# Attention's exponentials transposed by VectorE and a round trip through DRAM instead of by TensorE, for units 20 to 31

## The chip, the cores and the metric

The kernel runs on one core of one Trainium2 chip. The metric is the device time of one execution in microseconds, lower is better. Engines are named as in the profile: PE is TensorE's matrix multiply, PEld its weight load, DVE is VectorE, ACT is ScalarE, POOL is GpSimd, SP is SyncE, which issues all transfers of the kernel before.

## The reference

Three layers follow each other; all is float32 at the boundary. The change is in the first.

```python
# attention: q, k, v are (8 batches, 8 heads, 576 tokens, 64)
k_p = k.reshape(B, H, 72, 8, D).mean(axis=3)
v_p = v.reshape(B, H, 72, 8, D).mean(axis=3)
scores = scale * np.matmul(q, k_p.transpose(0, 1, 3, 2))
scores = scores - np.max(scores, axis=-1, keepdims=True)
attn = np.exp(scores)
attn = attn / (np.sum(attn, axis=-1, keepdims=True) + 1e-09)
attn_out = np.matmul(attn, v_p)
# first feed-forward layer: x is (4608 tokens, 512)
h = x @ w_in                                    # 512 -> 2048
g = np.where(h > 0.0, h, np.exp(np.minimum(h, 0.0)) - 1.0)
x1 = g @ w_out                                  # 2048 -> 512
# second layer: 512 -> 1024 -> 512, a softmax gate and a layer norm between
```

## The kernel before

**Attention** works in 32 units, one for each batch and pair of heads. Unit `i` is batch `i // 4`, pair `i % 4`; the two heads of a pair lie on 128 partitions. A unit from 4 on goes through these helpers. `att_setup` (L176) pools keys and values: DVE reduces (`att_kr`, `att_vr`, the latter into tile `vr`), ACT scales (`att_kc`, `att_vc`). `att_scores` (L183) multiplies five tiles of 128 queries, which start at the tokens in `QT` (0, 128, 256, 384 and 448, so that the last two overlap), by the pooled keys: ten PE instructions, into two PSUM banks. `att_max` (L206) takes the row maximum on DVE and subtracts it into the tile `es`, 128 queries by 10 groups (tile and head) by 72 keys. `att_exp` (L215) is one ACT instruction on 720 columns. `att_soft` (L229) sums and inverts on DVE and multiplies on POOL (L241). `att_T` (L243) transposes with PE against the identity: `att_T(i, 0)` four transposes of the first head (L251), `att_T(i, 1)` four of the second and the two of the last tile (L256); ACT copies the results from PSUM into `a`, 72 keys by 2 heads by 576 tokens (L252, L258). `att_V` (L262) multiplies by the pooled values (L277), in two pieces since a batch of 576 tokens crosses a block of 512, and `att_x` (L280) copies to `xr` and stores in DRAM (`x0d`).

**Order of the work.** The first feed-forward layer sets the pace. Its tokens are in nine blocks of 512. The first three are done straight, in slots `(j, f)` (functions `m_h1` to `m_o1`), each slot with a piece of `w_out` that ACT rounds (`woh`) and POOL subtracts (`wol`, L560). The other six blocks are done in three pairs with seven products instead of eight (`h_step`, L842; `mul_o`, L902): first the products with `w_in` (PE L818), then those with `w_out` (PE L908), their operands `op` prepared by ACT (L898) and DVE (L899), and the weights read by SP into a ring of 14 buffers (`wr`, L810). Between these pieces `att_half` (L369) issues attention by quarters of a unit: quarter 0 is scores, maximum and exponentials of unit `i`; quarter 1 its sums and product, and the second half of the transposes of unit `i - 1`; quarter 2 the product with the values of unit `i - 1` and the setup of unit `i + 1`; quarter 3 the first half of the transposes of unit `i`. Units 20 and 21 fall at the end of the third straight block and the start of the first pair, 22 to 27 into the first pair, 28 to 31 into the second. In all this stretch the program's scheduler may move instructions on each engine; every engine then runs its own list strictly in that order. The start (four units, first conversions of weights) and the second layer are ordered by hand.

Tiles come from pools: a tag has `bufs` buffers, and a tile that takes a buffer waits until all users of the tile before it there are done. `es` has 3 buffers, `a` 2, `vr` 2.

Of the kernel before, what the change touches and what calls it, by code (L numbers as in the profile page):

```python
# [8 lines left out]
F32 = mybir.dt.float32  # L9
# [11 lines left out]
def kernel(  # L21
# [41 lines left out]
    w3d = dr.tile([P, 7, NF // 2, 2, 256], F32, name="w3d")  # L63
    w2d = dr.tile([P, 7, 4, 512], F32, name="w2d")
    o2d = dr.tile([P, 2, 2, 4, 512], F32, name="o2d")
    zd = [dr.tile([4, P, 256], F32, name=f"zd{i}") for i in range(4)]
    ident = cst.tile([P, P], F32, name="ident")
    make_identity(nc, ident)
# [18 lines left out]

    GROUPED = (1, 2)
    NTREE = 3

    xh, xl = {}, {}
    gate = {}
# [71 lines left out]

    def att_vr(i):
        v_t = st["kq", units[i][1]][2] if i < NP else st["ld", i][1]
        vr = st["vr", i] = pa.tile([SK, P], F32, name=f"vr{i}", tag="vr")
        if i < NTREE:
            pool_tree(vr, v_t)
        else:  # L170
            nc.vector.tensor_reduce(vr, v_t, axis=AX, op=ALU.add)
# [8 lines left out]
    def bc(x, m):  # L180
        return x.rearrange("p (a o) -> p a o", o=1).to_broadcast([P, m, SK])

    def att_scores(i, banks):  # L183

        kp, vt = st["kp", units[i][0], units[i][1]]
        q_t = st.pop(("q", i))
        st["sv", i] = []
        for t0, t1 in ((0, 2), (2, 4)) if i < NP else ((0, 3), (3, 5)):
            s = next(banks)
            ts = QT[t0:t1]  # L190
            for t, o in enumerate(ts):
                nc.tensor.matmul(  # L192
                    s[:, t * 2 * SK:(t + 1) * 2 * SK], q_t[:, o:o + P], kp, start=True, stop=True
                )
            m = 2 * len(ts)
            st["sv", i].append((2 * t0, m, s[:, 0:m * SK].rearrange("p (a k) -> p a k", k=SK)))
            yield
        st["a", i] = (pa.tile([P, NG, SK], F32, name=f"es{i}", tag="es", bufs=3), vt)

    def grouped(i):  # L200
        return i in GROUPED
# [4 lines left out]
    def att_max(i):  # L206
        es, vt = st["a", i]
        mx = st["mx", i] = small(f"mx{i}")
        for g0, m, sv in st["sv", i]:
            mxs = mx[:, g0:g0 + m]  # L210
            nc.vector.tensor_reduce(mxs, sv, axis=AX, op=ALU.max, negate=grouped(i))
            if not grouped(i):
                nc.vector.tensor_tensor(es[:, g0:g0 + m, :], sv, bc(mxs, m), op=ALU.subtract)

    def att_exp(i):  # L215
# [27 lines left out]
    def att_T(i, h):  # L243

        es, vt = st["a", i]
        if h == 0:
            st["aT", i] = pa.tile([SK, 2, S], F32, name=f"a{i}", tag="a")
        a = st["aT", i]
        pt = ps.tile([P, 512], F32, name=f"pt{i}_{h}", tag="C")
        for t in range(4):  # L250
            nc.tensor.transpose(pt[0:SK, t * P:(t + 1) * P], es[:, 2 * t + h, :], ident)  # L251
        nc.scalar.copy(a[:, h, 0:4 * P], pt[0:SK, :])  # L252
        if h == 1 and i >= NP:
            pr = ps.tile([P, 512], F32, name=f"pr{i}", tag="C")
            for g in range(2):
                nc.tensor.transpose(pr[0:SK, g * P:(g + 1) * P], es[:, 8 + g, :], ident)  # L256
            lo = 5 * P - S
            nc.scalar.copy(  # L258
                a[:, :, 4 * P:S], pr[0:SK, 0:2 * P].rearrange("s (g t) -> s g t", g=2)[:, :, lo:P]
            )  # L260

    def att_V(i, banks):  # L262


        b, p = units[i]
        es, vt = st.pop(("a", i))
        a = st.pop(("aT", i))
        j = b * S // 512
        n = 512 * (j + 1) - b * S
        st["pv", i] = []  # L270
        for o, w, blk, at in ((0, n, j, b * S - 512 * j), (n, S - n, j + 1, 0)):
            if i < NP and o:
                continue
            pv = next(banks)
            for h in range(2):
                d = slice(64 * h, 64 * h + 64)
                nc.tensor.matmul(pv[d, 0:w], vt[:, d], a[:, h, o:o + w], start=True, stop=True)  # L277
            st["pv", i].append((pv[:, 0:w], blk, slice(at, at + w)))

    def att_x(i):  # L280
# [31 lines left out]
    def rest(part):  # L312

        kz = st["kz"]
        if part == 0:
            s = ps.tile([P, 512], F32, name="rs", tag="C")
            for p in range(NP):
# [1 line left out]
                    s[RW * (p % 2):RW * (p % 2) + RW, (p // 2) * 2 * SK:(p // 2 + 1) * 2 * SK],  # L319
                    kz[:, p, qr], kz[:, p, 0:2 * SK], start=True, stop=True,  # L320
                )
            es = st["rest"] = pa.tile([P, NG, SK], F32, name="esr", tag="es", bufs=3)[:, 0:NP]
            mx = small("mxr")[:, 0:NP]
            sv = s[:, 0:NP * SK].rearrange("p (a k) -> p a k", k=SK)
            nc.vector.tensor_reduce(mx, sv, axis=AX, op=ALU.max)
# [43 lines left out]
    def att_half(n):  # L369

        while nload[0] < min(NU, n // 4 + 3):
            att_load(nload[0])
            nload[0] += 1
        i, r = divmod(n, 4)
        before = NP <= i - 1
        if r == 0:
            if i < NU:
                for _ in att_scores(i, single()):
                    pass
                att_max(i)  # L380
                att_exp(i)
        elif r == 1:
            if i < NU:
                att_soft(i)
            if before:
                att_T(i - 1, 1)
        elif r == 2:
            if before:
                att_V(i - 1, single())
                att_x(i - 1)  # L390
            if i + 1 < NU:
                att_setup(i + 1)
        elif r == 3:
            if i < NU:
                att_T(i, 0)


# [1268 lines left out]
```

## Time and profile before

| | us |
|---|---|
| median of three runs (lowest, highest) | 1268.59 (1268.41, 1273.28) |
| profiled execution, own time | 1271.26 |
| its span in the trace | 1269.7 |
| PE busy | 1241.9 (98%) |
| PEld busy | 994.5 (78%) |
| DVE busy | 988.7 (78%) |
| ACT busy | 825.9 (65%) |
| POOL busy | 176.3 (14%) |

The span is the time from the first to the last instruction of the program on the slowest core; the execution's own time holds 1.6 us more that lies around it. Times inside the trace count from the start of the span. A matrix product's row shows how long one instruction took from start to end; they overlap in the pipeline, so the pace is read from the distance of starts. Between the third straight block and the last unit's product with the values lie 366 to 700 us.

### The profile page before, as it was taken

The numbers are of one execution on the slowest core, as the hardware profiler recorded it, in microseconds if no ns is written. First come the engines' busy times: TensorE is split into PE (matmuls) and PEld (weight loads), VectorE is DVE, ScalarE is ACT, GpSimd is POOL, SyncE is SP. The second block draws the span as 40 slices with busy tenths as digits, with TensorE's granted clock in tenths as the row PEclk, the third lists the DMA queues.
The fourth block names the chain that finished last, engine by engine and source line by source line (L and its number), as shares of the span: only waits on it lengthen the run. The fifth ranks groups of instructions, "written<-read, shape, count | busy, mean of one in ns | idle before, by whom it ended". The sixth has DMA issues, their size and how long they took to land.

```text
span 1269.7 us, 17261 instructions
## 1 busy us (share of the span) xinstructions
PE 1241.9 (98%) x5768; PEld 994.5 (78%) x5768; DVE 988.7 (78%) x1484; ACT 825.9 (65%) x1405; POOL 176.3 (14%) x148
## 2 busy tenths in 40 slices
PE   8999999999999999999999999999799999999998
PEld 6777877777777878788888777888688888888887
DVE  7898688978877799776795767986778787877763
ACT  7887566666656784557764477754667676767664
POOL 4564222333310001100000000000000000000000
PEclk8999999999999999999999999999899999999999
DMA  9976366665758877796666888878364444545451
GB/s 305 311 213 200 126 216 223 211 223 166 239 192 276 260 214 241 216 310 191 210 210 208 273 264 258 284 261 288 124 185 158 138 155 147 176 140 158 125 157 42
DMA packets 177065, 263.30 MB, mean 207 GB/s; under 512 B 16465, under 2 KB 96849, under 8 KB 175953
## 3 DMA queue, kind: packets, MB, share of 16 engines
q1 hardware_dynamic: 176976, 262.21, 65.0%
q8 instruction: 46, 0.75, 0.2%
q14 instruction: 43, 0.34, 0.1%
HBM read 182.46 MB, written 79.69 MB: 206 GB/s over the span
## 4 chain that ended last, share of the span: by engine, by line
PE 81%; DVE 8%; DMA 6%; ACT 3%; issue 1%; POOL 0%; SPq 0%; DVEq 0%; ACTq 0%; POOLq 0%
PE po L1138 15%; PE hA L818 13%; PE oA L908 12%; PE o L694 8%; PE h L639 8%; PE zX L1007 7%; PE zZ L1007 4%; PE at L192 3%; PE oB L908 3%; PE at L277 2%; PE hB L818 2%; PE pt L251 2%; PE zY L1007 2%; DMA w2d<-cv 1%; DMA x1r<-x1d 1%
## 5 line engine op out<-in xcount | busy, mean ns | idle before, releaser
L1138 PE MATMUL po<-w,dhl 128*128 128x512 f32 x864 | 204.5, 393 | 0.0
L908 PE MATMUL oA<-op,wr 128*128 128x512 f32 x864 | 202.4, 392 | 0.0
L908 PEld LDWEIGHTS oA<-op,wr 128*128 128x128 f32 x864 | 160.8, 188 | 38.1 <-issue 2.9
L1138 PEld LDWEIGHTS po<-w,dhl 128*128 128x128 f32 x864 | 162.7, 189 | 35.4
L898 ACT CAST op<-g 128x1024 fp32r<-128x1024 f32 x84 | 87.9, 1050 | 70.4 <-PE oA L908 32.2
L899 DVE TENSOR_TENSOR op<-g,op 128x1024 fp32r<-128x1024 f32 x84 | 102.8, 1231 | 33.8 <-ACT op L898 33.4
L818 PE MATMUL hA<-sS,wr 128*128 128x512 f32 x432 | 108.8, 394 | 1.8 <-ACT sp L830 1.8
L1007 PE MATMUL zX<-w,xh 128*128 128x512 f32 x288 | 100.9, 392 | 1.4 <-ACT sn L1017 1.4
L1086 POOL TENSOR_TENSOR sc<-sc,mhalf 128x1 f32<-128x1 f32 x36 | 19.3, 549 | 579.1 <-DVE sc L1085 344.1
L560 POOL TENSOR_TENSOR wol<-wo,woh 128x512 fp32r<-128x512 f32 x48 | 74.0, 1542 | 174.6 <-ACT woh L559 167.7
L818 PEld LDWEIGHTS hA<-sS,wr 128*128 128x128 f32 x432 | 79.9, 188 | 21.4 <-ACT sp L830 3.2
L241 POOL TENSOR_TENSOR es<-es,sm 128x720 f32<-128x720 f32 x28 | 48.2, 1722 | 304.9 <-DVE sm L239 137.1
L639 PE MATMUL h<-xh,wh 128*128 128x512 f32 x192 | 79.5, 414 | 2.4 <-DVE e L656 2.4
L838 DVE SCALAR_TENSOR_TENSOR g<-ep,g 128x512 f32<-128x512 f32 x72 | 50.9, 713 | 34.5 <-ACT ep L837 34.3
L694 PE MATMUL o<-gh,woh 128*128 128x512 f32 x192 | 77.6, 404 | 0.0
L639 PE MATMUL h<-xh,wl 128*128 128x512 f32 x192 | 76.2, 397 | 0.0
L639 PE MATMUL h<-xl,wh 128*128 128x512 f32 x192 | 76.2, 397 | 0.0
L694 PE MATMUL o<-gh,wol 128*128 128x512 f32 x192 | 75.0, 391 | 0.0
L1119 DVE TENSOR_TENSOR dhl<-dT,dhl 128x1024 fp32r<-128x1024 f32 x32 | 39.2, 1225 | 41.2 <-ACT dhl L1115 41.2
L1007 PEld LDWEIGHTS zX<-w,xh 128*128 128x128 f32 x288 | 54.0, 188 | 14.6 <-ACT sn L1017 2.1
L836 ACT ACTIVATE ep<-g 128x512 f32<-128x512 f32 x72 | 44.8, 628 | 25.6 <-DVE g L870 13.3
L892 DVE TENSOR_TENSOR g<-g,g 128x1024 f32<-128x1024 f32 x48 | 61.3, 1290 | 0.1
(354 smaller groups left out, 2736.8 us busy)
## 6 DMA issues: line engine op xcount, KB each, us to landing
wr<-w1d SPq DMA_DIRECT2D x168, 256.0 KB, 3.8
wr<-w3d SPq DMA_DIRECT2D x168, 256.0 KB, 2.9
raw<-in_w SPq DMA_DIRECT2D x48, 512.0 KB, 5.7
dT<-zd SPq DMA_DIRECT2D x128, 128.0 KB, 3.1
v<-in_v SPq DMA_DIRECT2D x32, 288.0 KB
x1r<-x1d SPq DMA_DIRECT2D x9, 1024.0 KB, 5.4
out<-ot SPq DMA_DIRECT2D x36, 256.0 KB, 2.0
w1d<-ci SPq DMA_DIRECT2D x16, 512.0 KB, 2.9
```

Of the source, the lines that this page charges most:

```text
L241: eng.tensor_tensor(es, es, bc(sm, n), op=ALU.mult)
L560: nc.gpsimd.tensor_tensor(ol, t[:, f % 4, :], oh.bitcast(F32), op=ALU.subtract)
L639: nc.tensor.matmul(h[:, 0:n], a[g][:, kk, fo:fo + P], x[j][:, kk, 0:n], start=(kk == 0 and m == 0), stop=(kk == KDM - 1 and m == 2), skip_ ...
L694: nc.tensor.matmul(acc, a[:, dm * P:(dm + 1) * P], x[:, 0:n], start=(f == 0 and m == 0), stop=(f == NF - 1 and m == 2))
L818: nc.tensor.matmul(bank, w[:, a, kk], x[:, b, kk], start=(start and m == 0), stop=(stop and m == 5), skip_group_check=True,)
L838: gate["dve"] = nc.vector.scalar_tensor_tensor(d, e, 1.0, h, op0=ALU.subtract, op1=ALU.max).ins
L892: nc.vector.tensor_tensor(d, x, y, op=op)
L898: gate["act"] = nc.scalar.copy(o[:, 0], src).ins
L899: gate["dve"] = nc.vector.tensor_tensor(o[:, 1], src, o[:, 0].bitcast(F32), op=ALU.subtract).ins
L908: nc.tensor.matmul(banks[d], ws[i][:, a, d * P:(d + 1) * P], o[:, b, i], start=(start and t == 0 and i == 0 and m == 0), stop=(stop and t ...
L1007: nc.tensor.matmul(bank, x[:, o:o + P], w[:, y + k, :], start=(start and m == 0), stop=(stop and m == 5), skip_group_check=True,)
L1138: nc.tensor.matmul(po, a[:, c], b[c // 4][:, c % 4, :], start=(m == 0), stop=(m == 3 * NC2 - 1))
```

## The change

For units from `BLOCKT = 20` on the transposes leave PE. `att_T` isn't called. The exponentials are laid out in `es` with the head outermost, padded from 720 to 736 columns (23 blocks of 32; POOL sets the last 16 to zero). A new `att_D` lets DVE transpose each block of 32 by 32 in place and has POOL issue four transfers, one for each 32 partitions, that store the blocks to one of four DRAM tiles `ed`, 736 rows of 128 queries, in runs of 32 numbers (128 bytes, 736 of them in each transfer). A new `att_A` has POOL issue one transfer back, 720 rows of 512 bytes, into `a` as 72 keys by 10 groups by 128 queries. `a` grows from 576 to 640 columns a head, the ACT copies go, and the query tiles are chosen so that no tile crosses the border of a block (`qtiles`). `vr` goes from two buffers to one, for all units.

```diff
+    ed = [dr.tile([736, P], F32, name=f"ed{i}") for i in range(4)]
...
+    BLOCKT = 20
...
-        vr = st["vr", i] = pa.tile([SK, P], F32, name=f"vr{i}", tag="vr")
+        vr = st["vr", i] = pa.tile([SK, P], F32, name=f"vr{i}", tag="vr", bufs=1)
...
+    def border(i):
+        o = units[i][0] * S
+        return 512 * (o // 512 + 1) - o
+
+    def qtiles(i):
+        if i < BLOCKT:
+            return QT
+        m = -(-border(i) // P)
+        return [P * t if t < m else S - P * (5 - t) for t in range(5)]
...
-            ts = QT[t0:t1]
+            ts = qtiles(i)[t0:t1]
...
-        st["a", i] = (pa.tile([P, NG, SK], F32, name=f"es{i}", tag="es", bufs=3), vt)
+        e = st["ef", i] = pa.tile([P, 736], F32, name=f"es{i}", tag="es", bufs=3)
+        st["a", i] = (e[:, 0:NG * SK].rearrange("p (g k) -> p g k", k=SK), vt)
...
-            if not grouped(i):
+            if i >= BLOCKT:
+                t = slice(g0 // 2, (g0 + m) // 2)
+                nc.vector.tensor_tensor(
+                    es.rearrange("p (h t) k -> p t h k", h=2)[:, t], sv.rearrange("p (t h) k -> p t h k", h=2),
+                    mxs.rearrange("p (t h o) -> p t h o", h=2, o=1).to_broadcast([P, m // 2, 2, SK]), op=ALU.subtract,
+                )
+            elif not grouped(i):
...
-            st["aT", i] = pa.tile([SK, 2, S], F32, name=f"a{i}", tag="a")
+            st["aT", i] = pa.tile([SK, 2, 5 * P], F32, name=f"a{i}", tag="a")
...
+    def att_D(i):
+
+        e = st.pop(("ef", i))
+        nc.vector.transpose(e, e)
+        for b in range(4):
+            nc.gpsimd.dma_start(
+                out=ed[i % 4][:, 32 * b:32 * b + 32].rearrange("(c f) j -> f c j", f=32),
+                in_=e[32 * b:32 * b + 32].rearrange("f (c j) -> f c j", j=32),
+            )
+
+    def att_A(i):
+        a = st["aT", i] = pa.tile([SK, 2, 5 * P], F32, name=f"a{i}", tag="a")
+        nc.gpsimd.dma_start(
+            out=a.rearrange("k h (t q) -> k (h t) q", q=P), in_=ed[i % 4][0:NG * SK].rearrange("(g k) q -> k g q", k=SK)
+        )
...
-                nc.tensor.matmul(pv[d, 0:w], vt[:, d], a[:, h, o:o + w], start=True, stop=True)
+                c = o + (64 if o and i >= BLOCKT else 0)
+                nc.tensor.matmul(pv[d, 0:w], vt[:, d], a[:, h, c:c + w], start=True, stop=True)
...
         if r == 0:
+            if i - 1 >= BLOCKT:
+                att_A(i - 1)
             if i < NU:
                 for _ in att_scores(i, single()):
                     pass
+                if i >= BLOCKT:
+                    nc.gpsimd.memset(st["ef", i][:, NG * SK:], 0.0)
...
-            if before:
+            if before and i - 1 < BLOCKT:
                 att_T(i - 1, 1)
         elif r == 2:
+            if BLOCKT <= i < NU:
+                att_D(i)
...
-            if i < NU:
+            if i < BLOCKT:
                 att_T(i, 0)
```

How the built programs stand on three engines shows what waits behind what. Line numbers are each program's own: in the changed one the scores are L204, the product with the values L313, the product on POOL L260, the transpose L284, the stores L286, the load L293.

**POOL, units 22 to 26, before** (`es_4273` is unit 23):

```order
L241 TENSOR_TENSOR es_4057<-es_4057,sm_4105 128x720
L241 TENSOR_TENSOR es_4273<-es_4273,sm_4315 128x720
L241 TENSOR_TENSOR es_4483<-es_4483,sm_4526 128x720
L241 TENSOR_TENSOR es_4697<-es_4697,sm_4767 128x720
L241 TENSOR_TENSOR es_4904<-es_4904,sm_4949 128x720
```

and in the changed program, units 23 to 26 (`es_4260` is unit 23, `es_4666` unit 25, `es_4864` unit 26; `ed_79` holds unit 25):

```order
L260 TENSOR_TENSOR es_4260<-es_4260,sm_4303 128x720
L286 DMA ed_81<-es_4260 32x23x32 x4
L293 DMA a_4452<-ed_81 72x10x128
L419 MEMSET es_4461 128x16
L260 TENSOR_TENSOR es_4461<-es_4461,sm_4505 128x720
L286 DMA ed_78<-es_4461 32x23x32 x4
L293 DMA a_4657<-ed_78 72x10x128
L419 MEMSET es_4666 128x16
L260 TENSOR_TENSOR es_4666<-es_4666,sm_4737 128x720
L286 DMA ed_79<-es_4666 32x23x32 x4
L260 TENSOR_TENSOR es_4864<-es_4864,sm_4910 128x720
L293 DMA a_4855<-ed_79 72x10x128
```

Each load stands behind its unit's four stores, whose landing it waits for, and ahead of the next unit's product; only for unit 25 does the product of unit 26 stand between its stores and its load.

**DVE, unit 23, before:**

```order
L236 TENSOR_REDUCE sm_4315<-es_4273 128x10
L838 SCALAR_TENSOR_TENSOR g_3777<-ep,g_3777 128x512
L238 TENSOR_SCALAR sm_4315<-sm_4315 128x10
L156 TENSOR_REDUCE kr_4996<-k_4684 128x72
L239 RECIPROCAL sm_4315<-sm_4315 128x10
L870 TENSOR_TENSOR g_3776<-hA,sp 128x512
L859 TENSOR_TENSOR g_3772<-hB,sp 128x512
```

and in the changed program:

```order
L255 TENSOR_REDUCE sm_4303<-es_4260 128x10
L880 SCALAR_TENSOR_TENSOR g_3787<-ep,g_3787 128x512
L257 TENSOR_SCALAR sm_4303<-sm_4303 128x10
L912 TENSOR_TENSOR g_3786<-hA,sp 128x512
L258 RECIPROCAL sm_4303<-sm_4303 128x10
L901 TENSOR_TENSOR g_3782<-hB,sp 128x512
L284 STREAM_TRANSPOSE es_4260<-es_4260 128x736
```

The transpose stands one instruction behind the inversion that POOL's product waits for, and itself waits for that product; the feed-forward layer's own work is queued behind it.

**PE, unit 25, before** (`a_4859` is unit 25's transposed tile, `es_4697` its exponentials):

```order
L192 MATMUL at<-kpbd_87,q_4472 128x144 x5
L908 MATMUL oB<-op,wr 128x512 x24
L251 MATMUL pt_1_4954<-ident,es_4697 72x128 x4
L256 MATMUL pr_4960<-ident,es_4697 72x128 x2
L908 MATMUL oB<-op,wr 128x512 x12
L277 MATMUL at<-a_4859,vt_4590 64x128 x2
L277 MATMUL at<-a_4859,vt_4590 64x448 x2
```

and in the changed program, where `a_4855` is what unit 25's load brings:

```order
L204 MATMUL at<-kpbd_91,q_4448 128x144 x5
L950 MATMUL oB<-op,wr 128x512 x36
L950 MATMUL oA<-op,wr 128x512 x18
L313 MATMUL at<-a_4855,vt_4564 64x128 x2
L313 MATMUL at<-a_4855,vt_4564 64x448 x2
```

The transposes are gone; the product with the values stands 18 matrix products later than before behind the scores of the next unit. For the other units of the first pair it keeps its place.

## Rows read from the trace of the kernel before

**Rows 1.** Stretches: us, then each engine's busy us, granted clock, DMA share, GB/s.

```profile
462.00:542.00 80.00, 80.00 (x393) 63.27 (x392) 70.29 (x85) 45.50 (x75) 8.94 (x4) 1.00 0.73 228
...
366.00:700.00 334.00, 332.07 (x1588) 264.73 (x1586) 257.65 (x331) 212.41 (x362) 19.47 (x11) 1.00 0.75 235
```

**Rows 2.** Waits of PE from 366 to 705: total us, times, longest.

```profile
PE hB L818 <- DVE sP L735: 0.6, 1, 0.6
```

**Rows 3.** PE in order of time: start us, us, instruction.

```profile
405.20 1.52 PE L818 MATMUL hB<-sP,wr 128*128 128x512 f32 x6
406.57 0.60 PE L251 MATMUL pt<-ident,es 128*72 128x128 f32 x4
...
407.14 1.64 PE L818 MATMUL hA<-sA,wr 128*128 128x512 f32 x6
408.61 1.53 PE L818 MATMUL hA<-sV,wr 128*128 128x512 f32 x6
...
416.81 0.60 PE L251 MATMUL pt<-ident,es 128*72 128x128 f32 x4
417.17 1.62 PE L818 MATMUL hB<-sP,wr 128*128 128x512 f32 x6
418.62 1.52 PE L818 MATMUL hA<-sA,wr 128*128 128x512 f32 x6
```

**Rows 4.** POOL in order of time, the products of units 23, 25 and 26.

```profile
430.24 1.40 POOL L241 TENSOR_TENSOR es<-es,sm 128x720 f32<-128x720 f32 x1 [20.43 <-DVE sm L239]
...
476.67 2.16 POOL L241 TENSOR_TENSOR es<-es,sm 128x720 f32<-128x720 f32 x1 [24.47 <-DVE sm L239]
490.82 2.16 POOL L241 TENSOR_TENSOR es<-es,sm 128x720 f32<-128x720 f32 x1 [11.98 <-ACT a L258]
```

**Rows 5.** PE in order of time, the products with the values of units 23 and 25.

```profile
451.71 1.19 PE L277 MATMUL at<-a,vt 72*64 72x192 f32 x8
...
492.32 1.19 PE L277 MATMUL at<-a,vt 72*64 72x128 f32 x8
```

**Rows 6.** DVE's block transposes in the second layer: duration ns min/median/max.

```profile
L1095 DVE STREAM_TRANSPOSE hb<-e x16: 1234/1236/1236, 916.6 to 1226.8; 128x1024 f32<-128x1024 f32 x16
```

**Rows 7.** SP's issue of a weight transfer of 128 rows: ns min/median/max.

```profile
L810 SPq DMA_DIRECT2D wr<-w1d x168: 319/320/1019, 369.2 to 789.0; - x168
```

**Rows 8.** Transfers by way of DRAM in the second layer: KB each, us to landing.

```profile
dT<-zd SPq DMA_DIRECT2D x128, 128.0 KB, 3.1
```

**Rows 9.** POOL's product of attention: ns min/median/max.

```profile
L241 POOL TENSOR_TENSOR es<-es,sm x28: 1392/1401/2892, 63.1 to 657.1; 128x720 f32<-128x720 f32 x28
```

**Rows 10.** DMA queue from 402 to 442: packets, MB, share of 16 engines.

```profile
q1 hardware_dynamic: 5303, 10.07, 82.8%
```

**Rows 11.** The same from 1000 to 1200.

```profile
q1 hardware_dynamic: 27550, 31.40, 50.6%
```

**Rows 12.** The start, DVE in order of time.

```profile
25.58 1.20 DVE L171 TENSOR_REDUCE vr<-v 72x128 f32<-72x1024 f32 x1
26.82 1.53 DVE L434 TENSOR_SCALAR wo<-wo 128x1024 uint32<-128x1024 uint32 x1
```

**Rows 13.** The start, ACT in order of time.

```profile
26.68 0.30 ACT L174 ACTIVATE kz<-vr 72x128 f32<-72x128 f32 x1
```

**Rows 14.** The start, PE in order of time.

```profile
39.67 0.50 PE L639 MATMUL h<-xh,wh 128*128 128x512 f32 x1 [2.37 <-DVE e L656]
```

**Rows 15.** The first pair's start, DVE in order of time.

```profile
375.99 0.22 DVE L239 RECIPROCAL sm<-sm 128x10 f32<-128x10 f32 x1
376.86 1.97 DVE L757 TENSOR_TENSOR sw<-sP,su 128x1024 f32<-128x1024 f32 x1 [0.65 <-DMA x1d<-x1s]
```

**Rows 16.** POOL behind unit 20's product, at 334 to 341.

```profile
334.06 1.46 POOL L241 TENSOR_TENSOR es<-es,sm 128x720 f32<-128x720 f32 x1 [1.35 <-DVE sm L239]
339.06 1.29 POOL L560 TENSOR_TENSOR wol<-wo,woh 128x512 fp32r<-128x512 f32 x1 [3.54 <-ACT woh L559]
```

**Rows 17.** PE where that piece of `wol` is first used.

```profile
346.34 0.39 PE L694 MATMUL o<-gh,wol 128*128 128x512 f32 x1
```

More of the change, by code (lines that the diff above doesn't have):

```diff
@@ L321, in rest @@
                 )
-            es = st["rest"] = pa.tile([P, NG, SK], F32, name="esr", tag="es", bufs=3)[:, 0:NP]
+            es = st["rest"] = pa.tile([P, 736], F32, name="esr", tag="es", bufs=3)[:, 0:NP * SK].rearrange("p (g k) -> p g k", k=SK)
             mx = small("mxr")[:, 0:NP]
```

## The prediction

> **What bounds the kernel now.** I read the stretches first: from 366 to 700 us, where the changed units lie, PE is busy 332.07 of 334 us [rows 1], so a PE instruction taken away there is time taken away, as long as PE doesn't wait for something new. Then the waits: what other engines cost PE there is small, 0.6 us at the first pair's start the only one that lasts beyond the transposes [rows 2]. DVE has room over the stretch as a whole (257.65 of 334 us) but little in the middle: 70.29 of 80 us from 462 to 542 [rows 1]. POOL is nearly idle, 19.47 us of 334.
>
> **What goes.** I read PE in order of time to see what transposes take from it, since their own durations overlap. Six matrix products take 1.37 us (405.20 to 406.57). Behind the six transposes at 406.57 the next six begin at 407.14, 0.57 later, and need 1.47 instead of 1.37, so these transposes cost 0.67. The four at 416.81 cost 0.36 (to 417.17) and again 0.08 in the products behind them, so 0.44 [rows 3]. A unit's ten cost 1.11 us. Twelve units lose them; unit 20's lie where PE is about to wait for DVE anyway, and I count eleven: **-12.2 us**.
>
> The Trainium skill (TensorE: Matmul & The Clock Gate, Part 4: PE-mode transpose) gives about 275 ns for one transpose inside a kernel. As an estimate, ten at that price would be 2.75 us a unit and eleven units 30 us. The rows agree with 275 ns only as one instruction's time from start to end and show 111 ns as what PE loses, so the trace decides.
>
> ACT's three copies a unit go as well. Nothing waits for ACT in the rows that bound the stretch, so I count nothing. The padding on POOL (16 columns) and the other order of the subtraction (the same columns on DVE) I count at nothing too; the cover is POOL's idle time and DVE's room, and if it is gone they cost what the rival on DVE says.
>
> **What is added: a chain that must end before PE reaches the product with the values.** POOL's product starts at 430.24 for unit 23 and PE's product with the values at 451.71, 21.5 us later [rows 4, 5]. Without the 1.1 us of transposes between them 20.4 are left. The new chain:
>
> - POOL's product, 1.40 us [rows 9].
> - DVE's transpose. The second layer's takes 1.236 us for 1024 columns [rows 6], so 736 columns take 0.89; with half a microsecond behind DVE's own work, 1.4.
> - Four issues on POOL of 736 descriptors each. No row shows POOL issuing a transfer. Below: SP's issue of 128 rows, 0.32 us [rows 7]. Above: POOL goes through 720 columns in 1.40 us [rows 9], 1.95 ns a step; were each of a descriptor's four words such a step, 736 would take 5.7, with SP's 0.32 on top 6.1 us. I take one step a descriptor, 1.44 + 0.32 = **1.75 us**, since the row on POOL itself is the nearest. Four take 7.0.
> - The stores' landing, as for the second layer's round trip, 3.1 us [rows 8]; the load's issue, 1.75; its landing, 3.1.
>
> Sum 1.4 + 1.4 + 7.0 + 3.1 + 1.75 + 3.1 = 17.75 us. It fits into 20.4 with 2.7 to spare. Unit 25 is the exception. Its load stands behind unit 26's product on POOL, which starts at 490.82 and takes 2.16 [rows 4]; with 1.75 and 3.1 the data land at 497.8. PE's product with the values stood at 492.32 [rows 5], 18 products at 0.228 us later in the new order, so 496.4, and 0.7 earlier for the transposes that no longer stand between it and unit 26's scores: 495.7. PE waits **+2.1 us** there. Behind POOL's issues nothing urgent is queued in the first pair: zeros for a later unit, then the next product 20 us on. In the second pair the distances are longer. At unit 20 it is the pieces of `wol` that are queued: POOL's product starts at 334.06, so with 1.4 for it and 1.4 for DVE the issues run from 336.9 to 343.9; the piece that began at 339.06 and took 1.29 ends at 345.2, and PE uses it at 346.34 [rows 16, 17]. That just holds.
>
> **DVE waits with the transpose.** It stands one instruction behind the inversion, so DVE idles for most of POOL's product, and everything behind it on DVE is late by up to 1.4 + 0.9. At the first pair's start it costs: the inversion of unit 21 ends at 376.21, POOL's product and the transpose then hold DVE until about 378.6, where before `sw` started at 376.86 and took 1.97 beside POOL's product [rows 15]. Alone it takes about 1.2, so it ends at 379.8 instead of 378.83, and less the 0.44 us by which the scores are earlier, PE's existing wait for what comes after it [rows 2] grows by 0.5 to 1: **+0.8 us**. Elsewhere DVE's work is prepared ahead of PE and I count nothing; the price without that is below.
>
> **One buffer for `vr`.** At the hand-ordered start the fourth unit's reduction on DVE (25.58) must now wait for ACT's scaling of the third, which ends at 26.98 [rows 12, 13], 1.4 us. DVE's conversions are queued behind it, and PE waits 2.37 us for their end until 39.67 [rows 14]. Between 0 and 1.4; since the conversion at 26.82 took 1.53 us beside POOL's work and may then be alone, I take **+1.0**.
>
> **The transfers** add 377 KB of stores in 2944 pieces and 369 KB of loads in 720 a unit. From 402 to 442 the queue moved 10.07 MB in 5303 packets with 82.8% of 640 engine-us, 52.6 ns a KB; from 1000 to 1200 a packet of 1.14 KB took 58.8 ns [rows 10, 11]. By bytes a unit adds 39 engine-us, 2.5 us of all sixteen; with each piece as dear as those packets, 13.5. Packet time goes with size in these two rows (99.9 ns for 1.9 KB), so I take 4 us, a share of 20% where 17% is free in the worst 40 us and more elsewhere. The ring of 14 weight buffers covers that; the price without it is below.
>
> **Sum:** -12.2 + 2.1 + 0.8 + 1.0 = **-8.3 us**. The profiled execution took 1271.3 us, its span 1269.7 and 1.6 around it, so 1263.0 by it. It stands 2.7 above the median of the runs, 1268.6, to which the forecast is made: **1260.3 us**.
>
> **The rivals.**
>
> *POOL's issues take longer, and PE waits at the product with the values.* This one ends slower. It decides from 2.2 us an issue, where the 2.7 us to spare are used up by five issues; every further microsecond makes a unit 5 us late, and as a wait gives the next unit its time back, about half is paid, 15 us over six units. At 2.8 the gain is gone. From 3.2 on it is slower by over 0.5%, and near 3 the issues, 5 x 3 with a landing and a product, also fill the 20 us from unit to unit. At 4 us POOL needs 24.5 a unit where 19.2 pass, 5.3 too much for six units: about +30, **1290 us**; at 6.1 us over 1340. For it: 736 descriptors are many, and no row bounds them well. Against: POOL does nothing else.
> The Trainium skill (DMA: Bandwidth & Descriptors, Anatomy of one DMA) calls descriptor generation a small, variable part of a fixed cost of about 2.0 us of a transfer from GpSimd; by that, issues would be well below 2 us and this rival would not occur. No run here shows it yet.
>
> *DVE becomes the bound from 462 to 542 us.* It has 9.7 us free there [rows 1]; four units add 0.89 each and a wait for POOL's product of up to the 2.16 it takes there [rows 4], 12.2 in all. About 2.5 us don't fit, and PE loses them, with as much again where a late operand holds ACT: **1265 us**, no change that can be told. For it: DVE's share. Against: PE waited for DVE only once there.
>
> *The small pieces fill the transfer engines, and weights come late.* At 8 us a unit, two units add 16 us to 40 us with 6.9 free; over six units some 15 us of PE's waits would be left after the ring has given what it has: **1275 us**. From about 5 us a unit on it decides.
> The Trainium skill (DMA: Bandwidth & Descriptors, Specifications) asks for 512 bytes at least, below which a transfer reads, modifies and writes; by that the pieces of 128 bytes would be dearer than their bytes. In the trace no store is so small, so it doesn't speak either way.
>
> **How the numbers follow.** Forecast 0.46; DVE bound 0.18; transfers 0.10; POOL's issues 0.26, half of it above 1290. The low end, 1253, is all twelve units' 13.3 us and up to 2 us of late work on ACT that goes, with none of the small losses. The high end, 1290, takes in the DVE and transfer cases and POOL's up to 4 us an issue; about 0.13 lies above and 0.04 below. Cases of both signs hold chances; the forecast's own range is 1255 to 1262. A measurement of this kernel can tell about 0.5%, 6.3 us, from no change. Faster by more than that: the forecast and a little of the rivals' better ends, 0.47. Within it: DVE's case, the milder transfer case and issues between 2.4 and 3.2 us, 0.27. Slower: 0.26.
>
> **What would show it.** Right: no L251 and L256 rows in the changed lines for units 20 on, PE's busy time down by some 12 us in the stretch, POOL's issues near 1.75 us, the product with the values without a wait except at unit 25, DVE idle 1 to 2 us ahead of each transpose. Wrong: PE waiting for the loads of `a` at L313 again and again (POOL's issues or slow landings), weights waiting on `wr` (transfers), or `op` late (DVE). The start is right if PE's first wait for `e` ends about 1 us later than 39.67.

## Result: 1.2% slower, and the profile after

The changed kernel takes 1285.05 us (median of four runs, 1281.62 to 1287.14) against 1268.61 of the kernel before beside it. The ratio is 1.0118, 95% interval 1.0086 to 1.0150: slower by 15 us, where 8 us less were forecast.

| | before, us | after, us |
|---|---|---|
| profiled execution, own time | 1271.26 | 1284.97 |
| its span | 1269.7 | 1283.0 |
| PE busy | 1241.9 | 1236.3 |
| DVE busy | 988.7 | 995.4 |
| ACT busy | 825.9 | 813.1 |
| POOL busy | 176.3 | 222.3 |

PE has less to do and the span is longer, so PE waits. The stretches, which answer to [rows 1] (columns as there: PE, PEld, DVE, ACT and POOL busy, granted clock, DMA share, GB/s):

```profile
462.00:542.00 80.00, 73.96 (x337) 57.29 (x336) 62.54 (x81) 38.61 (x60) 20.31 (x24) 0.96 0.87 253
366.00:700.00 334.00, 314.63 (x1413) 247.72 (x1413) 255.94 (x337) 194.05 (x318) 62.58 (x75) 0.98 0.84 253
```

PE idles 19.4 us of 334 where it idled 1.9. DVE is *less* busy from 462 to 542 than before (62.54 against 70.29), so DVE's capacity is not the bound. The DMA share rose from 0.75 to 0.84. PE's waits from 402 to 572, where before there were none at all (what was waited for, us in total, times, longest):

```profile
PE at L313 <- DMA a<-ed: 5.9, 3, 3.5
PE oA L950 <- ACT sp L872: 5.3, 1, 5.3
PE hA L860 <- ACT sp L872: 1.8, 2, 1.4
```

Setting equal PE products of the two traces side by side shows where the time goes: after is 1.8 us late at 331 us, 3.4 at 373, back to 1.5 at 441 (the transposes that are gone), 7.2 at 505, 14.1 at 543, 16.2 at 587, and 12.9 to 13.0 from 804 to the end. (Each is one start in after less the same product's in before.) So the first pair's second half loses it in two steps.

**First step, unit 25**, POOL and then PE in order of time, which answer to [rows 4, 5]:

```profile
480.42 2.18 POOL L260 TENSOR_TENSOR es<-es,sm 128x720 f32<-128x720 f32 x1 [13.03 <-ACT xr L327]
483.89 2.92 POOL L286 DMA_DIRECT2D ed<-es  x4 [1.28 <-DVE es L284]
493.28 2.18 POOL L260 TENSOR_TENSOR es<-es,sm 128x720 f32<-128x720 f32 x1 [6.47 <-DVE sm L258]
495.42 0.92 POOL L293 DMA_DIRECT2D a<-ed  x1
```

```profile
493.52 4.24 PE L950 MATMUL oA<-op,wr 128*128 128x512 f32 x18
501.27 2.19 PE L313 MATMUL at<-a,vt 72*64 72x128 f32 x8 [3.51 <-DMA a<-ed]
503.39 6.24 PE L950 MATMUL oA<-op,wr 128*128 128x512 f32 x18
```

The load stands behind unit 26's product, as the prediction had it, and PE waits 3.51 us. Then the same 18 products that took 4.24 us take 6.24, and the eight with the values 2.19 instead of 1.19 [rows 5]. The stretches around them show why (clock is the third column from the end):

```profile
496.00:499.00 3.00, 1.76 (x8) 1.13 (x6) 3.00 (x4) 0.00 (x0) 2.60 (x5) 1.00 0.69 182
501.30:503.50 2.20, 2.20 (x9) 0.80 (x9) 2.20 (x3) 0.27 (x1) 0.00 (x0) 0.50 0.47 110
503.50:506.00 2.50, 2.50 (x6) 2.04 (x7) 1.55 (x2) 0.74 (x2) 1.01 (x2) 0.50 0.33 102
```

After PE stood still the granted clock is 0.50, the lower level (1.2 of 2.4 GHz): the wait of 3.5 us costs 3.0 us more. The wait below does it again (granted clock 0.54 from 548 to 552): 90 products take 22.85 us behind it, where at the pace of the run's other products (36 in 8.48) they take 21.2.

**Second step, 534 to 547**, DVE, ACT and PE in order of time:

```profile
540.00 0.75 DVE L158 TENSOR_REDUCE kr<-k 128x72 f32<-128x576 f32 x1 [5.63 <-DMA k<-in_k]
540.66 0.21 DVE L258 RECIPROCAL sm<-sm 128x10 f32<-128x10 f32 x1
...
543.23 0.95 DVE L284 STREAM_TRANSPOSE es<-es 128x736 f32<-128x736 f32 x1 [1.28 <-POOL es L260]
544.10 1.18 DVE L934 TENSOR_TENSOR g<-g,g 128x1024 f32<-128x1024 f32 x1
```

```profile
545.37 1.04 ACT L940 CAST op<-g 128x1024 fp32r<-128x1024 f32 x1 [8.05 <-DVE g L934]
...
546.48 0.59 ACT L872 COPY sp<-oA 128x512 f32<-128x512 f32 x1
```

```profile
547.12 22.85 PE L950 MATMUL oA<-op,wr 128*128 128x512 f32 x90 [5.33 <-ACT sp L872]
```

DVE waits for keys (unit 31's, by the order of its list; PE needs them only after 650 us). SP issued that load at 530.30, so it took 9.7 us until DVE could start:

```profile
530.30 0.38 SPq L123 DMA_DIRECT2D k<-in_k  x1
```

Before, the loads of keys from 402 to 572 us landed in 3.4 to 4.0 us (min/median/max):

```profile
DMA to landing us min/median/max: 3.4/3.8/4.0
```

While the late load was under way the transfer engines were full, at a DMA share of 1.03 (columns as in the stretches above):

```profile
530.00:540.00 10.00, 9.04 (x44) 6.74 (x42) 4.33 (x9) 2.74 (x5) 0.00 (x0) 1.00 1.03 235
```

Behind this wait, on DVE, stand unit 28's inversion, the transpose with its wait for POOL's product, then the feed-forward layer's sums; ACT waits for those, and the copy that frees PE's bank is queued on ACT.

**The landing**, stores and loads of the whole execution (issue ns min/median/max; us to landing min/median/max), which answer to [rows 8]:

```profile
L286 POOL DMA_DIRECT2D ed<-es x48: 727/728/924, 338.6 to 679.3; - x48
...
DMA to landing us min/median/max: 2.8/4.3/7.1
```

```profile
L293 POOL DMA_DIRECT2D a<-ed x12: 883/893/917, 350.8 to 685.4; - x12
...
DMA to landing us min/median/max: 5.7/7.4/10.3
```

**The load on the transfer engines**, POOL's queue from 402 to 700 us, ten units (packets, MB, share of 16 engines), which answers to [rows 10]:

```profile
q0 software_dynamic: 3360, 7.47, 12.2%
```

### The profile page after: what moved, and what is told of

Read it like the earlier page. It is cut to its first block, busy times and chain, and to the rows that moved or that the text cites. A ratio compares the mean times of both kernels' runs of the same rounds, so it can differ in the third digit from the quotient of the medians.

```text
span 1283.0 us, 17134 instructions
## 1 busy us (share of the span) xinstructions
PE 1236.3 (96%) x5648; PEld 986.4 (77%) x5648; DVE 995.4 (78%) x1496; ACT 813.1 (63%) x1369; POOL 222.3 (17%) x220
## 4 chain that ended last, share of the span: by engine, by line
PE 69%; DVE 11%; DMA 10%; ACT 5%; issue 2%; POOL 1%; SPq 1%; ACTq 0%; DVEq 0%; POOLq 0%
PE po L1180 15%; PE oA L950 11%; PE hA L860 9%; PE zX L1049 7%; PE o L736 7%; PE h L681 6%; PE zZ L1049 4%; DMA raw<-in_w 3%; PE at L204 2%; PE zY L1049 2%; PE oB L950 2%; PE hB L860 2%; DMA x0d<-xr 2%; PE at L313 1%; DMA a<-ed 1%
## 5 line engine op out<-in xcount | busy, mean ns | idle before, releaser
L950 PE MATMUL oA<-op,wr 128*128 128x512 f32 x864 | 205.4, 397 | 6.5 <-ACT sp L872 5.3
L950 PEld LDWEIGHTS oA<-op,wr 128*128 128x128 f32 x864 | 164.2, 191 | 47.1 <-ACT sp L872 6.0
L260 POOL TENSOR_TENSOR es<-es,sm 128x720 f32<-128x720 f32 x28 | 46.5, 1660 | 222.9 <-DVE sm L258 180.9
L879 ACT ACTIVATE ep<-ep 128x512 f32<-128x512 f32 x96 | 59.4, 629 | 1.6
```

Of the source, the lines that this page charges most:

```text
L260: eng.tensor_tensor(es, es, bc(sm, n), op=ALU.mult)
L879: gate["act"] = nc.scalar.activation(e, e, AF.Exp, scale=-1.0).ins
L950: nc.tensor.matmul(banks[d], ws[i][:, a, d * P:(d + 1) * P], o[:, b, i], start=(start and t == 0 and i == 0 and m == 0), stop=(stop and t ...
```

## The experiments

Ratios are to the kernel before, run beside each on the same chip; us are the ratio less one times 1268.6.

### A ladder: one part of the change at a time

**vr1**, the kernel before with the one buffer:

```diff
-        vr = st["vr", i] = pa.tile([SK, P], F32, name=f"vr{i}", tag="vr")
+        vr = st["vr", i] = pa.tile([SK, P], F32, name=f"vr{i}", tag="vr", bufs=1)
```

> The kernel before with one buffer for vr and nothing else. Theory A (the loss lies in the transfers, the start costs what the trace of after shows): +1.8 us, 1270.4 us; PE's products with w_in near 128 us are about 1.7 us later than before and stay so. Rival B (one buffer costs nothing, the start's shift in the trace of after is chance): 1268.6 us, no shift.

Measured 1.0008 (0.9996 to 1.0021): +1.0 us, an interval that holds both nothing and 1.8 us. Against the trace of before, this run's PE products are 1.4 us late at 128 us but 0.1 early at 331, so the shift at the start does not stay.

**pe_only**, no transposes of any kind, no transfers:

```diff
-        e = st.pop(("ef", i))
-        nc.vector.transpose(e, e)
-        for b in range(4):
-            nc.gpsimd.dma_start(
...
+        st["ee", i] = st.pop(("ef", i))
...
-                nc.tensor.matmul(pv[d, 0:w], vt[:, d], a[:, h, c:c + w], start=True, stop=True)
+                src = st["ee", i][0:SK, 0:w] if i >= BLOCKT else a[:, h, c:c + w]
+                nc.tensor.matmul(pv[d, 0:w], vt[:, d], src, start=True, stop=True)
...
-            if i - 1 >= BLOCKT:
-                att_A(i - 1)
```

> The changed kernel without DVE's transposes and without stores and loads: for units 20 to 31 the product with the values reads the exponentials as they are, so what it computes there is not attention; PE, ACT, POOL's product and vr are as in the changed kernel. Prices the first term of the prediction: -12.2 us for the transposes with +1.8 for vr, so about 1258 us (theory A and rival B alike). If PE gains nothing from the missing transposes (rival C: PE then waits for operands), 1268 to 1271 us.

Measured 0.9915 (0.9898 to 0.9932): -10.8 us, with vr's 1.0 in it. PE's gain is 11.8 (by the two intervals 9 to 14.5); what goes along with the transposes, such as ACT's copies, is in it.

**plus_dve**, the transposes on DVE back:

> As the run without transposes, but DVE transposes the blocks in place behind POOL's product; still no stores and loads, the product with the values reads the tile that DVE transposed. Theory A: DVE's waits for POOL's product cost 1 to 4 us, 1259 to 1262 us. Rival B (the strict order on DVE behind POOL's product is the main loss): 1270 us or more.

Measured 0.9975 (0.9960 to 0.9989): -3.2 us. DVE's part costs 7.6 us (by the two intervals 4.8 to 10.4), between the two theories. Its trace shows the second step of above in small, DVE and PE:

```profile
525.00 0.75 DVE L158 TENSOR_REDUCE kr<-k 128x72 f32<-128x576 f32 x1 [2.30 <-DMA k<-in_k]
...
528.24 0.94 DVE L284 STREAM_TRANSPOSE es<-es 128x736 f32<-128x736 f32 x1 [1.28 <-POOL es L260]
```

```profile
532.13 13.22 PE L944 MATMUL oA<-op,wr 128*128 128x512 f32 x57 [2.04 <-ACT sp L866]
```

**plus_traffic**, the stores and loads back, but PE still reads what DVE transposed:

> As the run with DVE's transposes, and the stores and loads are issued as in the changed kernel, but nobody reads what the loads bring (the product with the values still reads the tile that DVE transposed). Theory A (the transfers hold up keys, weights and stores of other work): 8 to 14 us more than without them, 1268 to 1275 us, keys landing 6 to 10 us after their issue. Rival C (only PE's waits for its own loaded tile cost): within 2 us of the run without transfers, 1259 to 1264 us.

Measured 1.0083 (1.0062 to 1.0104): +10.5 us. The transfers cost 13.7 us (10 to 17) though no engine uses what they bring. The changed kernel's +15.0, in which PE also waits for the loaded tile, is 4.5 above that; the two intervals are too wide to tell this from nothing.

### Which part of the transfers

**traffic_no_dve**, transfers without DVE's transposes:

> As the run without transposes (the product with the values reads the exponentials as they are), but stores and loads are issued as in the changed kernel and read by nobody; DVE transposes nothing. Theory A (transfers cost by holding up lists whose engines also wait for POOL's product and the transpose): less than the 13.7 us that they cost beside DVE's transposes, 4 to 9 us, 1264 to 1269 us. Rival E (transfers cost the same by themselves): 13 us or more, 1272 to 1275 us.

Measured 1.0044 (1.0025 to 1.0063): +5.6 us, 16.4 above pe_only. Rival E held: the transfers don't need DVE's transposes to cost.

**stores_only** (no `att_A`) and **big_pieces**, both from plus_traffic:

```diff
-                out=ed[i % 4][:, 32 * b:32 * b + 32].rearrange("(c f) j -> f c j", f=32),
-                in_=e[32 * b:32 * b + 32].rearrange("f (c j) -> f c j", j=32),
+                out=ed[i % 4].rearrange("r q -> (r q)").rearrange("(p c) -> p c", c=736)[32 * b:32 * b + 32],
+                in_=e[32 * b:32 * b + 32],
```

> As the run with transfers that nobody reads, with the stores in small pieces but without the loads. Theory A1 (small pieces of the stores): 1276 to 1281 us. Theory A2 (bytes and loads): about half of the 13.7 us, 1272 to 1275 us. If the loads alone do it: 1267 us.

> As the run with transfers that nobody reads, but the four stores of a unit go out in 128 pieces of 2944 bytes instead of 2944 pieces of 128 bytes, same bytes; loads unchanged (what they bring is read by nobody in both). Theory A1 (the small pieces are what fills the transfer engines): most of the transfers' 13.7 us goes, 1267 to 1272 us, DMA share in the first pair near 0.80, keys landing in about 5 us. Theory A2 (the bytes and the loads do it): 1278 to 1282 us, DMA share 0.83 to 0.85 as with small pieces.

Measured 1.0025 (1.0011 to 1.0038) and 1.0055 (1.0039 to 1.0072). By these, the stores are worth 6.3 of the 13.7 us, the loads the rest. Pieces of 2944 bytes in place of 128 save 3.6 us, with an uncertainty as large (0 to 7), a time of 1275.6 us between the two theories. So about half of the price at least stays with the bytes and the loads, and what the small pieces cost is not shown. The Trainium skill (DMA: Bandwidth & Descriptors, Specifications) wants 512 bytes at least for full speed; the sign here would agree, but it is within the noise. The trace of before, of which the prediction said that it doesn't speak to this, does have small stores: those of `xr` in pieces of 256 bytes, 32 KB in all, landed in 2.6 us, those of 192 KB in pieces of 1536 bytes in 2.4.

**junk_pool, junk_half, junk_tiny**: pe_only with the transfers on POOL that nothing waits for (source a constant, loads of the unit before's rows), in full, in half (12 for 23, 5 groups loaded), and of 32 pieces each. Stores and loads stand on POOL behind the unit's product. The source of the full stores:

```diff
-                in_=e[32 * b:32 * b + 32].rearrange("f (c j) -> f c j", j=32),
+                in_=ident[32 * b:32 * b + 32, 0:32].rearrange("f (o j) -> f o j", o=1).to_broadcast([32, 23, 32]),
```

> The run without transposes (the product with the values reads the exponentials as they are), with as many stores and loads of the same sizes on POOL, whose data nobody waits for: the stores take a constant tile, the loads bring what the unit before stored. Rival E (transfers cost by being on the engines): 12 to 18 us more than without them, 1272 to 1278 us. Theory A (they cost by what waits for them in a list): under 6 us, 1260 to 1266 us.

> The transfers on POOL that nobody waits for, with half of the bytes and pieces (12 of 23 rows of blocks stored, 5 of 10 groups loaded), same number of issues at the same places. The full ones cost 22 us against the ones of 32 pieces. If the price goes with the load: 9 to 13 us of the 22, 1270 to 1274 us. If it starts only where the engines are full: under 4 us, 1261 to 1265 us.

> The same number of stores and loads on POOL at the same places, each cut to 32 pieces (4 KB stores, 16 KB loads). Rival E (bytes and pieces on the engines): within 2 us of the run without transfers, 1258 to 1262 us. If POOL's issuing or the queue's mere use costs: as much as with the full sizes, 1272 us or more.

Measured 1.0108 (1.0087 to 1.0129), 0.9988 (0.9973 to 1.0002) and 0.9933 (0.9913 to 0.9954): +13.7, -1.5 and -8.5 us. POOL's issuing costs little: 2.3 us above pe_only, within the intervals. Half the load costs 7.0 us, between the two theories, and all of it 22.2, so the price grows faster than the load. Above pe_only the full transfers cost 24.5 us, more than the 12 to 18 expected. The landing of SP's weights, the same transfers in all three, from 366 to 712 us (min/median/max), for junk_tiny, junk_half and junk_pool:

```profile
DMA to landing us min/median/max: 2.6/3.6/6.4
```

```profile
DMA to landing us min/median/max: 2.6/3.9/7.8
```

```profile
DMA to landing us min/median/max: 2.6/4.6/9.5
```

and the same stretch, columns as above:

```profile
366.00:712.00 346.00, 343.23 (x1565) 271.63 (x1564) 273.72 (x346) 209.79 (x337) 48.56 (x75) 1.00 0.79 249
```

```profile
366.00:712.00 346.00, 337.29 (x1528) 266.60 (x1528) 266.94 (x341) 205.59 (x333) 56.52 (x75) 0.99 0.81 251
```

```profile
366.00:712.00 346.00, 327.84 (x1463) 259.18 (x1462) 255.18 (x331) 198.93 (x325) 63.55 (x76) 0.98 0.83 250
```

The mean DMA share hardly moves (0.79, 0.81, 0.83) while the slowest landing goes from 6.4 to 9.5 us and PE's idle time from 2.8 to 18.2 (junk_pool's profiled execution is the longest of its six). Short stretches tell more than the mean: of the 43 of 8 us from 366 to 710, the share is 0.97 or more in 4 of junk_tiny, 6 of junk_half and 12 of junk_pool, and in 3 of before and 11 of after. It is no price by itself: traffic_no_dve's profiled execution has 16 of them and took 1268.5 us, the shortest of its twelve, whose longest is 1283.6.

What PE waited for in junk_pool, where nothing waits for the added transfers, shows whom they delay:

```profile
393.35 0.47 PE L864 MATMUL hB<-sP,wr 128*128 128x512 f32 x1 [2.25 <-DMA wr<-w1d]
434.78 2.56 PE L864 MATMUL hA<-sP,wr 128*128 128x512 f32 x6 [3.29 <-DVE g L884]
477.56 2.93 PE L864 MATMUL hA<-sS,wr 128*128 128x512 f32 x6 [5.85 <-ACT sp L876]
```

The first is for weights. The other two stand behind ACT's conversion of a weight piece (`cv`), whose buffer comes free only when the store of an `xr` has landed; the ACT rows, the two stores from issue to landing on the chain that ended last, and the stretches they were under way:

```profile
431.08 0.66 ACT L518 ACTIVATE cv<-raw 128x512 f32<-128x512 f32 x1 [4.45 <-DMA x0d<-xr]
...
475.33 0.66 ACT L518 ACTIVATE cv<-raw 128x512 f32<-128x512 f32 x1 [5.36 <-DMA x0d<-xr]
```

```profile
422.91 8.09 DMA x0d<-xr
...
467.37 7.88 DMA x0d<-xr
```

```profile
422.91:431.00 8.09, 8.09 (x42) 6.90 (x41) 2.08 (x3) 2.55 (x5) 0.00 (x0) 1.00 1.01 292
467.37:475.25 7.88, 4.34 (x24) 3.48 (x22) 3.37 (x5) 2.58 (x4) 0.00 (x0) 1.00 0.97 225
```

In junk_tiny ACT's waits of this kind come to 1.2 us. So the late operand is another one in each run (keys in after, this buffer here), and the full engines are what they share. The Trainium skill (DMA: Bandwidth & Descriptors, Issuing engines are not separate DMA queues) says that transfers of all issuing engines interleave on the same 16; these landings, SP's weights later the more POOL's queue moves, agree.

**junk_sp**, the same issued by SP:

> The same transfers issued by SP, each unit's behind its stores of xr. Theory F (POOL's queue is what makes them dear): at most half the price on POOL, 1264 to 1268 us. If the bytes and pieces are what costs: within 4 us of the run on POOL; above it only if SP's issues hold up the weights.

Measured 1.0254 (1.0231 to 1.0277): +32 us, 18.5 more than on POOL. PE waits 7.9 us for weights here, where it waited 2.2 in junk_pool, which fits the condition named for a time above: SP's list carries the weights too. The Trainium skill (DMA: Bandwidth & Descriptors, Issuing engine by pattern) calls SP's way generally faster. The kernel's time goes the other way, but this run shows the two placements, not the speed of the two queues alone. Packets from 366 to 712 in the run on POOL and the one on SP:

```profile
DMA packets 46296, 86.56 MB, mean 250 GB/s; under 512 B 6195, under 2 KB 8947, under 8 KB 46271
```

```profile
DMA packets 81373, 82.85 MB, mean 239 GB/s; under 512 B 37974, under 2 KB 47492, under 8 KB 81350
```

and POOL's queue alone (packets, MB, share of 16 engines):

```profile
q0 software_dynamic: 3696, 8.21, 10.9%
```

POOL's queue sent the 40304 pieces of these eleven units in 3696 packets, SP's about one each.

### Which waits

**v_late** and **d_late**, product with the values, and then the transpose too, one quarter later:

```diff
+    def later(i):
+        return BLOCKT <= i < NU and i not in (27, 31)
...
+            elif later(i):
+                att_D(i)
+            if before and later(i - 1):
+                att_V(i - 1, single())
+                att_x(i - 1)
```

The lines below the dots stand in quarter 3, and quarter 2 leaves these calls out for the same units; the two with `att_D` are in d_late alone.

> The changed kernel with the product with the values one quarter of a unit (some 5 us) later, except for units 27 and 31. Theory A: PE's waits for the loaded tile go (5.9 us in the trace, 4.5 us by the difference of the two runs), the rest of the loss stays: about 1280 us. If those waits only hid another one: 1284 us as the changed kernel.

> As the run with the late product with the values, and DVE's transpose and the stores one quarter later too (not for units 27 and 31), so that DVE need not wait for POOL's product. Theory A: most of DVE's 7.6 us goes for ten of twelve units, and PE's waits for the loaded tile come back in part since the data start 5 us later: 1274 to 1282 us. If DVE's loss is the transpose's own time and not its wait: 1284 us or more.

Measured 1.0120 (1.0099 to 1.0140) and 1.0125 (1.0089 to 1.0160): no gain shown from either, against theory A (d_late's interval reaches 1279.9 us, so a small one isn't excluded). d_late does only a part of what it was for: DVE's waits for POOL's product, in after and then in d_late (us in total, times, longest), do not go:

```profile
DVE es L284 <- POOL es L260: 11.2, 9, 1.6
```

```profile
DVE es L284 <- POOL es L260: 7.0, 5, 1.6
```

In v_late PE's wait for the tile falls to 1.56 us at 508, and others stand where there were none:

```profile
437.07 2.93 PE L867 MATMUL hA<-sS,wr 128*128 128x512 f32 x6 [4.34 <-ACT sp L879]
```

**kr_late** and **pins**:

```diff
+                with tc.issue_after(gate["tr"]) if i >= 28 else ExitStack():
+                    att_setup(i + 1)
...
+        with tc.issue_after(gate["ld_a"]) if i > BLOCKT else ExitStack():
+            eng.tensor_tensor(es, es, bc(sm, n), op=ALU.mult)
```

`gate["tr"]` is DVE's last transpose, `gate["ld_a"]` POOL's last load; the second order is in pins alone.

> The changed kernel with one more order on DVE: the setup of units 29, 30 and 31 (sums of keys and values) is queued behind the transposes of units 28, 29 and 30; in the changed kernel the sum of unit 31's keys stands ahead of unit 28's inversion near 540 us and waits 5.6 us for its keys, though they are used at 660 us. Theory A (the late keys hold DVE's list, and behind it POOL's product, the transpose and the feed-forward layer's operands): PE's wait of 5.3 us near 542 us goes, 4 to 8 us less, 1277 to 1281 us. Rival D (the stall there comes from the weights or stores themselves): 1284 us or more.

> As the run with the later setup, and POOL's product of each unit from 21 on is queued behind the load of the unit before, which changes the order at unit 25 and 26 alone. Theory A: PE's wait of 3.5 us for unit 25's tile falls to under 1 us, 2 to 5 us less than the run with the later setup alone, 1273 to 1279 us. If the wait is covered by another one: the same as that run.

Measured 1.0077 (1.0048 to 1.0105) and 1.0090 (1.0063 to 1.0118). With the keys moved, PE doesn't wait from 534 to 560, and all 96 products follow each other:

```profile
535.18 22.06 PE L951 MATMUL oA<-op,wr 128*128 128x512 f32 x96
```

So that chain is shown; that it is worth the 5 us less is not, since the intervals of the two kernels are too wide. In pins unit 25's product with the values starts without a wait, and the next unit's waits instead:

```profile
496.56 1.19 PE L314 MATMUL at<-a,vt 72*64 72x128 f32 x8
516.64 1.41 PE L314 MATMUL at<-a,vt 72*64 72x128 f32 x8 [4.49 <-DMA a<-ed]
```

### Can it win anywhere

**bt28** (`BLOCKT = 28`), **bt28_vr2** (also two buffers for `vr`, and `a` in 576 columns) and **bt28_kr** (that with kr_late's order):

> The changed kernel with BLOCKT = 28, nothing else changed: four units in the second pair, vr with one buffer, one load a unit. Theory E (the load of the transfers costs where the engines are busy, and four units carry a third of it): between -0.3% and +0.2%, 1267 to 1273 us. If the price lay in the first pair alone: -0.3% or better, 1266 us or less.

> The change for units 28 to 31 alone, where 35 us and more lie between POOL's product and the product with the values, with two buffers for vr as before and the loaded tile in 576 columns (three loads a unit instead of one). Theory A: 4 x 1.1 us less on PE, less about 1 us of waits on DVE, and no price at the start: 1264 to 1267 us. If transfers or DVE cost there as much as in the first pair: 1270 us or more.

> The change for units 28 to 31 alone with two buffers for vr, and the setup of units 29 to 31 queued behind the transposes of units 28 to 30. Theory A: 2 to 4 us less than without that order, 1266 to 1269 us, at best 0.3% faster than the kernel before. If keys were no matter there: 1270 to 1271 us.

Measured 1.0026 (1.0010 to 1.0042), 0.9991 (0.9977 to 1.0005) and 1.0019 (1.0004 to 1.0034). None beats the kernel before; bt28_vr2 lies between its two theories (1267.5 us), and moving the keys there brought nothing.

## Why the prediction was wrong

- **PE's transposes, -12.2 us: right.** pe_only gives 11.8. The distance of starts was the right measure, not an instruction's own time.
- **The transfers, 0 us ("The ring of 14 weight buffers covers that"): this step failed.** Measured 13.7 us beside DVE's transposes, 16.4 and 22.2 without. The load itself was sized well: POOL's queue takes 12.2% of 16 engines from 402 to 700 us in the trace of after, 3.6 us of all sixteen a unit against 4 taken. What failed is the cover. The ring covers weights, and PE waits for them in none of the rows of after above, for 2.2 us in junk_pool and 7.9 in junk_sp. Keys, the loaded tile and stores whose landing frees a buffer have no such ring. They land late while the engines are full (keys 9.7 us at a share of 1.03, stores of `xr` 8.1 and 7.9 at 1.01 and 0.97), and one late operand stops a strictly ordered list. The third rival had the right resource and a price near the measured one (15 us), but for 8 us of engine time a unit, and with weights as the victim.
- **DVE, +0.8 us at one place and nothing elsewhere ("Elsewhere DVE's work is prepared ahead of PE"): failed too.** Measured 7.6 us. The rival on DVE looked at its room, which was not used up. The rows of plus_dve and after show a chain of order instead: inversion, POOL's product, transpose, and the feed-forward layer behind. That this order makes up the 7.6 us is argued and not shown, since d_late left most of DVE's waits in place. At the first pair's start the term held: PE's wait [rows 2] went from 0.6 to 1.21 us.
- **One buffer for `vr`, +1.0: not told from nothing.** vr1 gives the same +1.0, but between -0.5 and +2.7, and its shift at the start is gone by 331 us, so the agreement is luck as far as is known. In the trace of after the place is right: the reduction starts at 26.98 behind ACT's scaling instead of 25.58 [rows 12]. But PE's first product behind DVE's conversions comes at 40.12 instead of 39.67 [rows 14], 0.45 us later and not the 1 us that was named as the sign.
- **Unit 25, +2.1: the wait was there**, 3.51 us and 3.0 more at the lower clock. But pins, which takes it away, is no faster: the next unit waits. At unit 20 the cover held: at 349 us PE waits 0.97 us for ACT's operand `gh` and not for the piece of `wol`.
- **The chain of 17.75 us: near by two errors that cancel, which is luck.** Five issues took 3.8 us, not 8.75; the two landings 11.7, not 6.2. Rival one, slow issues on POOL, fell at 0.73 and 0.89 us. The Trainium skill (DMA: Bandwidth & Descriptors, Anatomy of one DMA) had the issues cheap, and the trace agrees. By the fixed cost of about 2.0 us and the rate for the bytes that the Trainium skill gives in the same section, an estimate is 2.2 us for a store and 2.8 for a load, far below the landings of 4.3 and 7.4 seen here.
- **The sum** of the ladder, in us: -11.8 + 1.0 + 7.6 + 13.7 + 4.5 = +15.0; each term is the difference of two runs, so it must come out. In the profiled execution about 4.7 us are the lower clock behind two waits, a term that the prediction didn't have.

Left open: how much the waits for the tile cost by themselves (4.5 us, uncertain by as much), what of DVE's part is its order, and in what order the full engines served a load of keys so that it took 9.7 us.

## What to carry to other kernels

A transfer nobody waits for is not free where the transfer engines are 75% busy: look for stretches of a few microseconds in which they are full, ask which other transfers, stores that free a buffer too, have no ring of buffers, and what stands behind their readers on a strictly ordered engine. Work moved off the bounding engine by way of DRAM pays in landings, so price it by landings seen at that load, not in a quiet stage. Removing one PE wait in such a stretch gained nothing by itself; the wait moved to the next unit.

## What was not expected of the hardware

- A wait of PE of 3.5 or 5.3 us left the granted clock at 0.50 for the products behind it, 3.0 and some 1.7 us more; waits of 1.4 us did not.
- POOL issues 736 pieces of 128 bytes in 0.73 us, and its queue sent 40304 pieces in 3696 packets; SP's queue sent the same pieces as packets of their own. The kernel took 1.4% longer than with POOL, but there PE waited 7.9 us for weights too, against 2.2.
- The mean share of busy time of the DMA engines told little: 0.79 to 0.83 went with -8.5 to +13.7 us. The stretches of 8 us at 0.97 or more went from 4 to 12.
